# Attention, routed experts and a second expert layer in one kernel: where ak's copy, the routing steps, the low parts of the first weights and the last batch's routing chain are issued

## The chip, the cores and the metric

The kernel runs on one core of one Trainium2 chip. The time is the device time of one execution in microseconds. Its engines are TensorE (PE: matmuls and transposes; its weight loads, PEld, overlap them), VectorE (DVE), ScalarE (ACT), GpSimd (POOL) and SyncE (SP), which here only issues transfers (DMAs). Each engine works through its own instructions in order and waits on semaphores for the others.

## The reference

All inputs are float32. Three stages follow each other; the token of a batch is a row of 512 values (8 heads x 64).

```
# 1. attention with decay: batch 4, heads 8, seq 576, head_dim 64
scores = q @ k.T / 8 + cum[:, None] - cum[None, :]     # cum = cumsum(log(clip(f, 1e-4, 1)))
scores = where(causal, -1e9, scores);  attn = exp(scores - max)
x = (attn / (attn.sum() + 1e-9)) @ v                   # -> 2304 tokens x 512
# 2. one of 8 experts for each token (w1: 512 x 1024, w2: 1024 x 512)
logits = x @ w_gate + modality_bias[modality_id];  e = argmax(logits)
p = exp(logits - max);  gate = (p / (p.sum() + 1e-9))[e]
y = gate * (relu(x @ w1[e]) @ w2[e])
# 3. a dense layer, 2048 wide
h = y @ w_in;  out = maximum(0.01 * h, h) @ w_out
```

## The kernel before

**Precision.** Each float32 operand of a matmul is split into a high part (a copy in the type fp32r) and a low part (the operand less its high part). A product is three matmuls: high x high, high x low, low x high. For an expert's weights `parts(which, k)` makes both: ScalarE copies (`w1h`, `w2h`), VectorE subtracts (`w1l`, `w2l`).

**Attention** runs over 16 head pairs g = 0 to 15, four to a batch. Each pair has five chunks of 128 query rows (the last of 64) and passes through `first`, `last`, `third`, `fourth`. `first(g)` computes the scores of chunks 0 and 1 (`qk01`), transposes the exponentials of chunk 3 of the pair before, prepares the next pair and takes the exponentials of chunks 0 and 1. `last(g)` does chunk 4's scores (`qk4`), `tr(g - 1, 4)`, and attention times values `pv(g - 1, 0)`; `third(g)` chunk 2 and `pv(g - 1, 1)`; `fourth(g)` chunk 3 and the output stage `xout(g - 1)` (two matmul groups into PSUM, normalised by VectorE into `x` and into the gate's partial logits `lp`). Scores lie in the PSUM pool `psc` with two buffers; a chunk's scores can start when the exponentials of two chunks earlier have read theirs. Transposes and output share the pool `pst` with three buffers. `psv`, which `pv` writes and VectorE empties into `xu` and `xub`, has one.

**Preparing a pair.** `raw` holds q (partitions 0 to 63) and k (64 to 127). `prep_hi(g + 2)` rounds both to `aq`, in `fourth(g)`. `prep_lo(g + 1)`, in `first(g)`, copies the high part of k from `aq[64:128]` to `ak[0:64]` (ScalarE), subtracts the low parts (VectorE), and moves 288 KB each by DMA: low q to `bq`, low k to `ak[64:128]`, and the high q from `aq[0:64]` to `aq[64:128]` (which the copy must have read). `qk01(g + 1)` needs all of them. SP issues these in program order, with the stores of finished token rows to `xs` (`store`), the loads of later pairs and those of weights.

**Routing.** When a batch's four pairs are done, `route(b)` (batches 0 to 2) computes each token's expert, gate and rank within its expert, in pieces: it is a generator, each `yield` ends a piece, and `plan` says at which place of which pair the next piece is issued. `route1` (key B) does the table of the first four slots of 128 tokens, and the gathers `xg` of slots 0 and 1. `late_route` is batch 3's. `finish` makes the table of the remaining slots.

**Drain and experts.** `drain(15)` finishes pair 15 and begins slot 0: `wload(0, ...)`, `trx` (transpose a slot's tokens, split into `xh`, `xl`), `gemm1`, `keep` (relu). Then `step(t)` runs over the slots t: `gemm1(t)` and `gemm2(t - 1)` with the weights of the next slot split beside them. Slots 1 to 3 load and split weights only if their expert differs from the slot before (`tc.If`, L1008, a branch that ScalarE and VectorE take). `side` lists what `aside(t, place)` issues between the parts of a step. `gather(K1)`, K1 = 4, belongs to `finish`.

**Order.** `ordered(tc, engines)` keeps program order on the engines named (all five in attention and in the steps). Instructions of two such blocks that follow each other may still be mixed by the scheduler where one runs into the next, as are drain and step 0. `tc.issue_after(i)` queues the block's instructions of i's engine behind i.

Of the kernel before, what the change touches and what calls it, by code (L numbers as in the profile page):

```python
# [19 lines left out]
P = 128  # L20
# [54 lines left out]
def fused(ctx: ExitStack, tc, qk0, qk2, vp, f, mid, wg, mb, w1, w2, w_in, w_out, out):  # L75
# [93 lines left out]

    def parts(which, k):  # L170
        raw, hi, lo = (w2r, WL["2h"], WL["2l"]) if which else (w1r, w1h, WL["1l"])
        nc.scalar.copy(hi[k], raw[k])  # L172
        nc.vector.tensor_tensor(lo[k], raw[k], hi[k].bitcast(F32), ALU.subtract)  # L173
# [25 lines left out]
    with tc.tile_pool(name="pst", bufs=PST, space=PSUM) as pst:  # L199
# [161 lines left out]
        def prep_lo(g):  # L361
            raw, aq, ak = ops[g]
            bq, bk, b4 = bqs[g % NBUF], bks[g % NBUF], bq4[g % NBUF]
            h = aq.bitcast(F32)
            nc.scalar.copy(ak[0:64], h[64:128])
            nc.vector.scalar_tensor_tensor(raw.bitcast(F32R), raw, qs, h, ALU.mult, ALU.subtract)
            nc.sync.dma_start(bq[0:64].bitcast(F32), raw[0:64])
            nc.sync.dma_start(ak[64:128].bitcast(F32), raw[64:128])
            preps.append(nc.sync.dma_start(h[64:128], h[0:64]))
            nc.gpsimd.tensor_copy(b4[0:64, :, :64], raw[0:64, :, 4 * P:])  # L370
            ops[g] = (aq, bq, ak, bk)
# [177 lines left out]
        def route(b):  # L549
# [17 lines left out]
            nc.vector.tensor_tensor(eq, L, mx.unsqueeze(2).to_broadcast(shp), ALU.is_equal)  # L567
            nc.gpsimd.tensor_tensor(lm, L, mx.unsqueeze(2).to_broadcast(shp), ALU.subtract)
            nc.gpsimd.tensor_tensor(eq, eq, rev.unsqueeze(1).to_broadcast(shp), ALU.mult)
            yield  # L570
# [42 lines left out]
        def late_route(b):  # L613
# [18 lines left out]
            nc.vector.tensor_tensor(lm, L, mx.unsqueeze(2).to_broadcast(shp), ALU.subtract)  # L632
# [138 lines left out]
        for b in range(B - 1):  # L771
            a = 4 * b + 5
            places = [(a - 1, "end"), (a, "first")]
            if b < B - 2:
                places += [(a, "idle"), (a, "fourth"), (a + 1, "third"), (a + 1, "idle"), (a + 2, "idle")]
            else:
                places += [(a, "last"), (a, "after"), (a, "third"), (a, "idle"), (a + 1, "idle")]
            for k in places:
                plan.setdefault(k, []).append(b)
        for k in ((13, "end"), (14, "last"), (14, "third"), (15, "first"), (15, "after")):  # L780
            plan.setdefault(k, []).append(B)
# [6 lines left out]
        def first(g):  # L788
            then = qk01(g) if g < NG else None
            cs = [tr(g - 1, 3, (j, )) for j in range(2)] if g else ()  # L790
            for c in cs:
                c()
            if g + 1 < NG:
                prep_lo(g + 1)
# [8 lines left out]
        def last(g):  # L803
            then = qk4(g) if g < NG else None
            if g:
                tr(g - 1, 4, (0, 1))
                routed(g, "last")
# [33 lines left out]
        def drain(g):  # L841
            for k in range(4):
                wload(0, 1, k)
            tr(g, 4, (0, 1))
            for c in [tr(g, 3, (j, )) for j in range(2)]:
                c()
            parts(0, 2)
            pv(g, 0)
            trx(0, pst, "t")
            pv(g, 1)  # L850
            parts(0, 3)
            for k in range(4):
                wload(1, 0, k)
            gemm1(0, 0, 2, psc, "sc")
            xout(g)
            gemm1(0, 2, 3, psc, "sc")
            next(routing[B - 1])
            trx(1, pst, "t")
# [3 lines left out]
        with ordered(tc, MS):  # L862
            prep_hi(1)
            for g in range(NG):
# [23 lines left out]
                if g == NG - 1:  # L888
                    parts(0, 0)
                routed(g, "idle")  # L890
                fourth(g)
                if g == NG - 1:
                    parts(0, 1)
# [87 lines left out]
    with tc.tile_pool(name="rt2", reuse_waits="tile", bufs=1) as rt2, \  # L981
# [87 lines left out]
        def step(t):  # L1069
            nx = t + 1 < NS  # L1070
            if not t:
                split(t, 1, 0)
                split(t, 1, 1)
# [115 lines left out]
        for k, w in (((0, "load"), late), ((0, "b"), late), ((0, "d"), late), ((1, "load"), fini), ((1, "load"), fini), ((1, "a1"), late), ((1, "b"), fini), ((1, "pool"), late), ((1, "d"), fini), ((2, "b"), fini)):  # L1189
# [150 lines left out]
```

## Time and profile before

| | |
|---|---|
| three runs | 889.17, 890.4, 894.68 us; median 890.4 |
| profiled execution | 894.38 us; its span, first to last instruction, 892.7 us; mean granted TensorE clock 0.987 |
| busy, share of the span | PE 96%, DVE 66%, ACT 57%, POOL 20% |
| attention, drain, experts, dense layer | about 0 to 210, 210 to 230, 230 to 482, 482 to 893 us (their edges overlap) |

Times within the profile are counted from the span's start. "Idle before" is the time that an engine stood still ahead of an instruction, with what released it. A granted clock of 1.00 is 2.4 GHz for TensorE, 0.50 is 1.2 GHz. A line number such as L399 is that of the kernel before.

### The profile page before, as it was taken

The page shows a single profiled execution, that of the slowest core. Times are in us where ns is not written, and L with a number is a line of the kernel's source. Part 1 is how long each engine was busy: PE and PEld are TensorE (multiplying, and loading weights), DVE is VectorE, ACT ScalarE, POOL GpSimd, SP SyncE. Part 2 cuts the span into 40 slices and gives each one's busy share as a digit, 9 for nine tenths or more (in the row PEclk, how much of TensorE's full clock was granted, in tenths as well). Part 3 has the DMA queues.
Part 4 walks back from the last instruction along what each step waited for, and adds up shares of the span by engine and source line. Part 5 has one row for each costly group of instructions (what it writes and reads, how often), then busy time and mean ns, then how long its engine had stood idle before and what let it go on. Part 6 is the DMA issues. An engine that isn't in the chain of part 4 may idle for free. (4 is left out here: it accounts for less than half of the span.)

```text
span 892.7 us, 14386 instructions
## 1 busy us (share of the span) xinstructions
PE 854.7 (96%) x4733; PEld 709.8 (80%) x4733; DVE 586.7 (66%) x978; ACT 506.0 (57%) x969; POOL 181.5 (20%) x308
## 2 busy tenths in 40 slices
PE   4999999998899999999999999999999999999996
PEld 3888778886788888888877788888888888888885
DVE  6576667775737999999986373387337853473333
ACT  6777877876247999999975253453223422242221
POOL 5002122251226345444441000000000000001112
PEclk9899999999899999999999999999999999999998
DMA  5676786875268336211421240032001300011111
GB/s 158 199 180 179 193 213 165 218 180 208 78 185 279 96 116 202 67 46 62 119 95 46 78 134 21 1 96 94 0 1 48 119 24 0 1 48 48 48 48 70
DMA packets 33603, 92.92 MB, mean 104 GB/s; under 512 B 7957, under 2 KB 8629, under 8 KB 33522
## 3 DMA queue, kind: packets, MB, share of 16 engines
q1 hardware_dynamic: 28690, 76.70, 29.5%
q0 software_dynamic: 4800, 15.23, 5.0%
q8 instruction: 39, 0.64, 0.3%
q14 instruction: 42, 0.34, 0.1%
q10 hardware_dynamic: 32, 0.01, 0.0%
HBM read 132.09 MB, written 14.99 MB: 165 GB/s over the span
## 5 line engine op out<-in xcount | busy, mean ns | idle before, releaser
L1232 ACT COPY us<-u 128x512 f32<-128x512 f32 (+1 forms) x80 | 43.6, 545 | 162.7 <-PE u L1230 162.6
L1233 DVE SCALAR_TENSOR_TENSOR us<-u,us 128x512 f32<-128x512 f32 (+1 forms) x80 | 51.0, 637 | 126.7 <-ACT us L1232 124.3
L1230 PE MATMUL u<-fxl,whii 128*128 128x512 f32 (+1 forms) x320 | 118.0, 369 | 0.0
L1230 PE MATMUL u<-fxh,wloi 128*128 128x512 f32 (+1 forms) x320 | 117.9, 368 | 0.0
L1230 PE MATMUL u<-fxh,whii 128*128 128x512 f32 (+1 forms) x320 | 116.9, 369 | 0.7 <-ACT fxh L932 0.7
L1250 PE MATMUL a<-whio,gh 128*128 128x512 f32 x280 | 109.7, 392 | 0.0
L1250 PE MATMUL a<-wloo,gh 128*128 128x512 f32 x280 | 109.2, 390 | 0.0
L1250 PE MATMUL a<-whio,gl 128*128 128x512 f32 x280 | 103.2, 390 | 0.0
L173 DVE TENSOR_TENSOR w1l<-w1r,w1h 128x1024 fp32r<-128x1024 f32 x72 | 86.9, 1225 | 16.5 <-ACT w1h L172 16.3
L1260 POOL DMA_INDIRECT out<-acc,tid x18 | 17.8, 987 | 326.7 <-DVE acc L1257 288.0
L173 DVE TENSOR_TENSOR w2l<-w2r,w2h 128x1024 fp32r<-128x1024 f32 x68 | 80.3, 1219 | 0.6 <-ACT w2h L172 0.4
L399 ACT ACTIVATE p<-sc,nm 128x128 f32<-128x128 f32 (+3 forms) x128 | 66.1, 525 | 23.1 <-DVE nm L394 21.1
L1235 ACT CAST gh<-us 128x512 fp32r<-128x512 f32 (+1 forms) x76 | 44.6, 587 | 57.0 <-DVE us L1233 38.1
L172 ACT CAST w1h<-w1r 128x1024 fp32r<-128x1024 f32 x72 | 74.0, 1054 | 1.5 <-PE h L190 1.5
L1236 DVE TENSOR_TENSOR gl<-us,gh 128x512 fp32r<-128x512 f32 (+1 forms) x76 | 49.2, 648 | 37.4 <-ACT gh L1235 35.2
L394 DVE TENSOR_REDUCE nm<-sc 128x2 f32<-128x256 f32 (+1 forms) x64 | 51.0, 817 | 31.7 <-PE sc L390 25.0
L172 ACT CAST w2h<-w2r 128x1024 fp32r<-128x1024 f32 x68 | 69.4, 1051 | 2.6 <-PE y L1037 1.3
L1230 PEld LDWEIGHTS u<-fxh,whii 128*128 128x128 f32 x320 | 60.2, 188 | 11.0 <-ACT fxh L932 0.9
L1230 PEld LDWEIGHTS u<-fxh,wloi 128*128 128x128 f32 x320 | 60.3, 188 | 10.4
L1230 PEld LDWEIGHTS u<-fxl,whii 128*128 128x128 f32 x320 | 60.3, 188 | 10.4
L1037 PE MATMUL y<-w2h,hh 128*128 128x512 f32 x160 | 64.5, 403 | 0.0
L1037 PE MATMUL y<-w2h,hl 128*128 128x512 f32 x160 | 62.8, 393 | 0.0
(318 smaller groups left out, 1854.2 us busy)
## 6 DMA issues: line engine op xcount, KB each, us to landing
w1r<-w SPq DMA_DIRECT2D x88, 512.0 KB
w2r<-w SPq DMA_DIRECT2D x82, 512.0 KB
rwi<-w_in SPq DMA_DIRECT2D x16, 512.0 KB
rwo<-w_out SPq DMA_DIRECT2D x16, 512.0 KB
raw<-qk SPq DMA_DIRECT2D x14, 576.0 KB
vt<-vp SPq DMA_DIRECT2D x16, 320.0 KB
xr<-yd SPq DMA_DIRECT2D x18, 256.5 KB
bk<-aq SPq DMA_DIRECT2D x15, 288.0 KB
```

The lines of the kernel that those rows point to most:

```text
L172: nc.scalar.copy(hi[k], raw[k])
L173: nc.vector.tensor_tensor(lo[k], raw[k], hi[k].bitcast(F32), ALU.subtract)
L394: nc.vector.tensor_reduce(nm, view, axis=AX.X, op=ALU.max, negate=True)
L399: st["exp"] = nc.scalar.activation(pt[:, j, :], view[:, j, :], AF.Exp, bias=nm[:, j:j + 1], scale=1.0, accum_out=sms[g % 3][:, c, j:j + 1])
L1037: nc.tensor.matmul(Yp[t], lhsT=ap[:, k * P:(k + 1) * P], rhs=wp[k // 2][:, k % 2, :], start=(k == 0 and i == 0), stop=(k == NFB - 1 and i ...
L1230: nc.tensor.matmul(ps, lhsT=w[:, c], rhs=x[:, k, :], start=(k == 0 and i == 0), stop=(k == NKB - 1 and i == 2))
L1232: nc.scalar.copy(us, ps)
L1233: nc.vector.scalar_tensor_tensor(us, ps, 0.01, us, ALU.mult, ALU.max)
L1235: nc.scalar.copy(gh, us)
L1236: nc.vector.tensor_sub(gl, us, gh.bitcast(F32))
L1250: nc.tensor.matmul(A[b][i], lhsT=x[:, c], rhs=w, start=(first and m == 0), stop=(last and m == 2))
L1260: d = nc.gpsimd.indirect_dma_start(out=out[:, :], out_offset=bass.IndirectOffsetOnAxis(ap=tid[:, c:c + 1], axis=0), in_=Y[b, i], in_offset ...
```

## The change

Four parts. ak's copy and the DMA within `aq` leave `prep_lo` for `prep_k`, which for pairs 2 to 14 is issued in `last`, behind the exponentials of chunks 0 and 1 and the copies of chunk 4. In `route`, `eq x rev` goes from GpSimd to VectorE, a `yield` goes, and the places in `plan` are set anew. `parts` is cut into `high` and `low`; in `drain` the low parts are issued behind the output stage and `pv(15, 0)` ahead of chunk 3's transposes; `trx(1)` comes ahead of the last batch's first routing piece. The first two splits of w2 are queued behind the end of that piece on VectorE, and the pieces of `late_route` and `finish` get later places in `side`.

```diff
--- before.py
+++ after.py
@@ -167,10 +167,20 @@
         n = NTOK if t >= K1 else NTOK - S
         nc.gpsimd.indirect_dma_start(out=xg[t % 2], out_offset=None, in_=xs[:n, :], in_offset=bass.IndirectOffsetOnAxis(ap=m[:, i:i + 1], axis=0), bounds_check=n - 1, oob_is_err=False)
 
+    def tiles(which, k):
+        return [t[k] for t in ((w2r, WL["2h"], WL["2l"]) if which else (w1r, w1h, WL["1l"]))]
+
+    def high(which, k):
+        raw, hi, _ = tiles(which, k)
+        nc.scalar.copy(hi, raw)
+
+    def low(which, k):
+        raw, hi, lo = tiles(which, k)
+        nc.vector.tensor_tensor(lo, raw, hi.bitcast(F32), ALU.subtract)
+
     def parts(which, k):
-        raw, hi, lo = (w2r, WL["2h"], WL["2l"]) if which else (w1r, w1h, WL["1l"])
-        nc.scalar.copy(hi[k], raw[k])
-        nc.vector.tensor_tensor(lo[k], raw[k], hi[k].bitcast(F32), ALU.subtract)
+        high(which, k)
+        low(which, k)
 
     def trx(t, pool, tag):
         ps = pool.tile([P, 512], F32, tag=tag, name=f"tx{t}")
@@ -362,13 +372,17 @@
             raw, aq, ak = ops[g]
             bq, bk, b4 = bqs[g % NBUF], bks[g % NBUF], bq4[g % NBUF]
             h = aq.bitcast(F32)
-            nc.scalar.copy(ak[0:64], h[64:128])
             nc.vector.scalar_tensor_tensor(raw.bitcast(F32R), raw, qs, h, ALU.mult, ALU.subtract)
             nc.sync.dma_start(bq[0:64].bitcast(F32), raw[0:64])
             nc.sync.dma_start(ak[64:128].bitcast(F32), raw[64:128])
+            nc.gpsimd.tensor_copy(b4[0:64, :, :64], raw[0:64, :, 4 * P:])
+
+        def prep_k(g):
+            raw, aq, ak = ops[g]
+            h = aq.bitcast(F32)
+            nc.scalar.copy(ak[0:64], h[64:128])
             preps.append(nc.sync.dma_start(h[64:128], h[0:64]))
-            nc.gpsimd.tensor_copy(b4[0:64, :, :64], raw[0:64, :, 4 * P:])
-            ops[g] = (aq, bq, ak, bk)
+            ops[g] = (aq, bqs[g % NBUF], ak, bks[g % NBUF])
 
         st = {}
         XA, XB = 3 * P, P + 64
@@ -565,9 +579,8 @@
             eq = t3("eq")
             lm = t3("lm")
             nc.vector.tensor_tensor(eq, L, mx.unsqueeze(2).to_broadcast(shp), ALU.is_equal)
+            nc.vector.tensor_tensor(eq, eq, rev.unsqueeze(1).to_broadcast(shp), ALU.mult)
             nc.gpsimd.tensor_tensor(lm, L, mx.unsqueeze(2).to_broadcast(shp), ALU.subtract)
-            nc.gpsimd.tensor_tensor(eq, eq, rev.unsqueeze(1).to_broadcast(shp), ALU.mult)
-            yield
             m2 = rsp.tile([P, NC], F32, tag="m2", name=f"m2{b}")
             red(m2, eq, ALU.max)
             oh = oall[:, b * NC:(b + 1) * NC, :]
@@ -629,7 +642,7 @@
             nc.vector.tensor_tensor(eq, eq, rev.unsqueeze(1).to_broadcast(shp), ALU.mult)
             nc.vector.tensor_reduce(m2, eq, axis=AX.X, op=ALU.max)
             nc.vector.tensor_tensor(oh, eq, m2.unsqueeze(2).to_broadcast(shp), ALU.is_equal)
-            nc.vector.tensor_tensor(lm, L, mx.unsqueeze(2).to_broadcast(shp), ALU.subtract)
+            st["late"] = nc.vector.tensor_tensor(lm, L, mx.unsqueeze(2).to_broadcast(shp), ALU.subtract)
             yield
             rk = ranks(b, oh, pmx, "tx")
             yield
@@ -770,14 +783,14 @@
         plan = {}
         for b in range(B - 1):
             a = 4 * b + 5
-            places = [(a - 1, "end"), (a, "first")]
+            places = [(a - 1, "end"), (a, "idle" if b < B - 2 else "first")]
             if b < B - 2:
-                places += [(a, "idle"), (a, "fourth"), (a + 1, "third"), (a + 1, "idle"), (a + 2, "idle")]
+                places += [(a, "end"), (a + 1, "third"), (a + 1, "idle"), (a + 2, "idle")]
             else:
-                places += [(a, "last"), (a, "after"), (a, "third"), (a, "idle"), (a + 1, "idle")]
+                places += [(a, "last"), (a, "third"), (a, "idle"), (a + 2, "first")]
             for k in places:
                 plan.setdefault(k, []).append(b)
-        for k in ((13, "end"), (14, "last"), (14, "third"), (15, "first"), (15, "after")):
+        for k in ((13, "end"), (14, "idle"), (14, "idle"), (15, "last"), (15, "after")):
             plan.setdefault(k, []).append(B)
 
         def routed(g, at):
@@ -788,9 +801,12 @@
         def first(g):
             then = qk01(g) if g < NG else None
             cs = [tr(g - 1, 3, (j, )) for j in range(2)] if g else ()
+            if g < 2:
+                prep_lo(g + 1)
+                prep_k(g + 1)
             for c in cs:
                 c()
-            if g + 1 < NG:
+            if 2 <= g < NG - 1:
                 prep_lo(g + 1)
             store(1 + (g > 12))
             routed(g, "first")
@@ -804,6 +820,8 @@
             then = qk4(g) if g < NG else None
             if g:
                 tr(g - 1, 4, (0, 1))
+                if 2 <= g < NG - 1:
+                    prep_k(g + 1)
                 routed(g, "last")
                 pv(g - 1, 0)
             if then:
@@ -841,21 +859,27 @@
         def drain(g):
             for k in range(4):
                 wload(0, 1, k)
+            low(0, 0)
             tr(g, 4, (0, 1))
-            for c in [tr(g, 3, (j, )) for j in range(2)]:
+            high(0, 1)
+            pv(g, 0)
+            low(0, 1)
+            cs = [tr(g, 3, (j, )) for j in range(2)]
+            for c in cs:
                 c()
-            parts(0, 2)
-            pv(g, 0)
             trx(0, pst, "t")
+            high(0, 2)
             pv(g, 1)
-            parts(0, 3)
+            low(0, 2)
+            high(0, 3)
+            gemm1(0, 0, 2, psc, "sc")
+            low(0, 3)
             for k in range(4):
                 wload(1, 0, k)
-            gemm1(0, 0, 2, psc, "sc")
             xout(g)
             gemm1(0, 2, 3, psc, "sc")
+            trx(1, pst, "t")
             next(routing[B - 1])
-            trx(1, pst, "t")
             gemm1(0, 3, 4, psc, "sc")
             keep(0)
 
@@ -886,11 +910,9 @@
                 if not g:
                     last(g)
                 if g == NG - 1:
-                    parts(0, 0)
+                    high(0, 0)
                 routed(g, "idle")
                 fourth(g)
-                if g == NG - 1:
-                    parts(0, 1)
                 routed(g, "end")
             drain(NG - 1)
         att.close()
@@ -1069,8 +1091,9 @@
         def step(t):
             nx = t + 1 < NS
             if not t:
-                split(t, 1, 0)
-                split(t, 1, 1)
+                with tc.issue_after(st["late"].ins):
+                    split(t, 1, 0)
+                    split(t, 1, 1)
             keepg(t)
             if t + 2 < NS and t + 2 != K1:
                 gather(t + 2)
@@ -1186,7 +1209,7 @@
 
         fini = finish()
         late = routing[B - 1]
-        for k, w in (((0, "load"), late), ((0, "b"), late), ((0, "d"), late), ((1, "load"), fini), ((1, "load"), fini), ((1, "a1"), late), ((1, "b"), fini), ((1, "pool"), late), ((1, "d"), fini), ((2, "b"), fini)):
+        for k, w in (((1, "load"), late), ((1, "b"), late), ((1, "pool"), late), ((1, "pool"), late), ((1, "d"), fini), ((1, "d"), fini), ((2, "load"), late), ((2, "load"), fini), ((2, "b"), fini), ((2, "d"), fini)):
             side.setdefault(k, []).append(w)
         with ordered(tc, MS2):
             for t in range(NSTAT):
```

## Rows read from the trace of the kernel before

**Rows 1.** The page's first part: engine, busy us, share of the span, instructions.
```profile
PE 854.7 (96%) x4733; PEld 709.8 (80%) x4733; DVE 586.7 (66%) x978; ACT 506.0 (57%) x969; POOL 181.5 (20%) x308
```

**Rows 2.** TensorE's waits, whole span: for what, us in total, times, longest.
```profile
PE sc L384 <- ACT p L399: 7.3, 13, 0.6
...
PE rk L605 <- DVE oall L631: 1.7, 1, 1.7
...
PE pv L485 <- DVE xu L491: 1.4, 2, 0.9
...
PE h L190 <- DVEq L1008: 0.7, 1, 0.7
```

**Rows 3.** Stretches: length, busy time by engine, granted clock, DMA share, GB/s.
```profile
22.90:29.75 6.85, 6.85 (x32) 6.58 (x32) 3.80 (x5) 3.52 (x10) 0.86 (x3) 0.50 0.93 293
190.14:193.55 3.41, 1.91 (x18) 1.60 (x18) 1.99 (x5) 1.94 (x8) 2.69 (x11) 1.00 0.95 223
...
214.07:217.49 3.42, 3.17 (x14) 1.63 (x14) 1.46 (x2) 2.71 (x6) 0.00 (x0) 0.50 0.02 5
...
231.09:237.92 6.83, 6.10 (x19) 4.74 (x18) 5.57 (x23) 1.03 (x4) 5.28 (x11) 0.50 0.16 42
...
233.00:445.00 212.00, 212.00 (x1032) 175.09 (x1031) 188.91 (x242) 173.56 (x232) 92.20 (x77) 0.99 0.39 123
```

**Rows 4.** TensorE's timeline, pairs 7, 8, 15, drain: start, us, instruction, idle before.
```profile
104.62 0.44 PE L384 MATMUL sc<-ak,aq 128*128 128x384 f32 x1 [0.56 <-ACT p L399]
...
110.88 0.30 PE L384 MATMUL sc<-ak,aq 128*128 128x128 f32 x1
...
197.88 0.32 PE L384 MATMUL sc<-ak,aq 128*128 128x128 f32 x1
...
213.19 0.41 PE L463 MATMUL pt<-ident,p 128*128 128x128 f32 x2 [2.33 <-DVE lp L512]
...
226.16 0.60 PE L178 MATMUL tx<-ident,xg 128*128 128x128 f32 x4
```

**Rows 5.** ScalarE's timeline in pair 7.
```profile
101.68 1.15 ACT L365 CAST ak<-aq 64x1152 fp32r<-64x1152 f32 x1
...
104.36 0.21 ACT L399 ACTIVATION_READ_ACCUMULATOR p<-sc,nm 128x1 f32 x1
104.45 0.76 ACT L465 COPY tt<-pt 128x384 f32<-128x384 f32 x2
```

**Rows 6.** SP's timeline in pair 14: transfers as they are issued.
```profile
190.56 0.71 SPq L369 DMA_DIRECT2D aq<-aq  x1
191.32 1.20 SPq L672 DMA_DIRECT2D xs<-x  x1
192.57 1.05 SPq L670 DMA_DIRECT2D xs<-x  x1
```

**Rows 7.** Stretches of pairs 7, 8 and 14 (columns as in rows 3).
```profile
104.00:110.00 6.00, 5.44 (x49) 4.55 (x48) 3.45 (x9) 4.42 (x16) 0.00 (x0) 1.00 0.98 239
116.00:122.50 6.50, 5.93 (x55) 4.86 (x52) 2.81 (x4) 4.92 (x16) 0.00 (x0) 1.00 0.96 234
190.00:198.30 8.30, 6.80 (x62) 5.92 (x58) 5.21 (x17) 5.76 (x19) 5.66 (x24) 1.00 0.99 249
```

**Rows 8.** VectorE's timeline in pair 13.
```profile
177.56 0.20 DVE L530 TENSOR_REDUCE mx<-lgs 128x5 f32<-128x40 f32 x1 [0.95 <-POOL lgs L561]
...
178.92 0.55 DVE L491 COPY xu<-pv 128x384 f32<-128x384 f32 x1
```

**Rows 9.** VectorE's timeline from pair 15's last scores into the first expert.
```profile
209.27 1.23 DVE L173 TENSOR_TENSOR w1l<-w1r,w1h 128x1024 fp32r<-128x1024 f32 x1 [2.09 <-ACT w1h L172]
210.41 1.22 DVE L394 TENSOR_REDUCE nm<-sc 128x2 f32<-128x1024 f32 x1
...
225.61 0.80 DVE L625 TENSOR_REDUCE lgs<-lp 128x40 f32<-128x320 f32 x1
...
232.31 0.34 DVE L645 TENSOR_SCALAR jall<-pf 128x5 f32<-128x5 f32 x1 [0.89 <-DVEq L1008]
```

## The prediction

> **What bounds the kernel now.** I read the page's first part, then what TensorE waited for, then busy time and clock by stretch, then the timelines of the four places that the diff touches. TensorE is busy for 854.7 of 892.7 us [rows 1], so an edit can pay only where TensorE stands still or runs at the lower clock. From 233 to 445 us it has no gap (212.00 of 212.00 busy) [rows 3]: a later start there would not be made up, and an earlier one is kept down to the end, VectorE (188.91 of 212) following. Ahead of it lie 13 short waits on the exponentials, 7.3 us together, one of about a microsecond on `xu`, one of 2.33 us in the drain, and 1.7 and 0.7 us when the experts begin [rows 2, 4]. Three stretches run at a granted clock of 0.50, that is at 1.2 GHz: 6.85, 3.42 and 6.83 us [rows 3]. Each comes behind one TensorE wait of 1.7 to 2.4 us; the waits of 0.55 and 0.95 us together, inside 190.14 to 193.55, were followed by none (1.00 there).
>
> **ak's copy behind the exponentials.** In pair 7 the exponentials of chunks 0 and 1 end at 104.36 + 0.21 = 104.57, and `qk(7, 2)` starts at 104.62 after 0.56 idle, so it was wanted at 104.06 [rows 4, 5]. With the copy (1.15, with its gap 1.17) taken from ahead of them they end at 103.40: the wait goes whole. Late next on ScalarE would be the fourth exponential: after the two copies of chunk 4 (0.76, to 104.2) and ak's copy (to 105.35) it ends near 106.4, and its PSUM buffer is wanted at 107.84 - 0.56 = 107.3. Covered by 0.9. Pairs 0 and 1 keep the copy ahead and show no such wait. Pairs 2 to 12: 11 x 0.56 = 6.2 us saved. Pairs 13 and 14 follow below.
>
> With the copy moves a DMA: the high part of q, 288 KB, into `h[64:128]`, for the next pair. It must wait for ScalarE's copy, so it now leaves SP at 105.4 or later, about a microsecond behind its old place; and in `first` the store of routed rows is now issued ahead of it on the same queue. Where there is no store it has 4.9 us till the next pair, and is hidden (a microsecond later is a microsecond of slack gone, no more). In pairs 7, 8, 11 and 12 a store of 513 KB goes ahead: 3 x 288 + 513 = 1377 KB, or 1.41 MB, must have moved. At 239 GB/s from 104.0 [rows 7] that is 109.9, against a need at 110.88 - 0.56 = 110.32 [rows 4]; in pair 8, at 234 GB/s from 116.0, 122.0 against about 122.5. What the last pieces need beyond that I can't see. Bounds: 0 and 0.56 each (the old start); I take 0.25: 4 x 0.25 = 1.0 lost.
>
> Pair 14 is the bad one. There both stores (1026 and 128 KB) are issued behind the old place of the copy [rows 6], and now ahead of it. All four transfers are 3 x 288 + 1154 = 2018 KB = 2.07 MB, and 249 GB/s over 8.30 us from 190.0 [rows 7] is just that: the last lands at 198.3 or later. `qk01(15)` started at 197.88 and, with both waits of pair 14 gone (0.55 and 0.95), is wanted at 196.4. Bounds of the new wait: 0 (the copy overtakes the stores) and 3 us. I take 2.3, nearest to the byte count plus some tail: pair 15 starts at 198.7, which is 0.8 later than before, in place of 1.5 earlier.
>
> **Routing in one step, and the new places.** For batches 0 and 1 the five small VectorE steps move to "idle", behind `xub` and ahead of the next maxima, where VectorE waits for TensorE anyway (1.5 us in pair 8, which has no step of routing). They cost 5 x 0.22 = 1.1: nothing; with the cover gone it would be 1.1 each. In batch 2 they stay at (13, "first"), ahead of the chunk-4 maximum (0.75) and of `xu`. There VectorE waits 0.95 for GpSimd's logits and begins at 177.56; now mx, eq, eq x rev, m2 and oh run as one chain to 178.6, the maximum to 179.3, `xu` to 179.85, where it ended at 178.92 + 0.55 = 179.47 [rows 8]. TensorE, 0.57 earlier at that point, waits at `pv` for it: pair 13 saves nothing and loses 0.35. Batch 3's table: steps 2 and 3 leave (14, "last") for (14, "idle"), which takes VectorE's wait for GpSimd from ahead of `xu`; that is the 0.95 counted in pair 14. The five `lall` operations go from (14, "idle") to (15, "first"), 0.9 us that end before the chunk-4 scores are there: nothing. SP reads `ei` for the first expert's weights when GpSimd has written it, and that chain doesn't move.
>
> **Drain.** VectorE sits 2.09 us behind `w1h`, subtracts (1.23), and only then takes pair 15's last maxima (at 210.41) [rows 9]. The scores are there at 208.65, so without `low(0, 0)` ahead of it the maxima and pair 14's output stage behind them run 1.75 us earlier, and TensorE's 2.33 us wait [rows 4], which is for that output stage's PSUM buffer, shrinks to 0.6. The low parts that follow have 1.2 us each against gemm1 steps of 1.4 and come in time by my reckoning (the fourth by 3 us). From 213.19 to the transposes of the second tile's end at 226.5 are 13.3 us; less 0.74 of short waits and 1.6 for the half clock at 214.07 to 217.49 (3.17 busy) [rows 3, 4], 11.0. So `trx(1)` ends at 213.19 - 1.75 + 11.0 + 0.3 (for `tt`) = 222.7, 3.8 earlier.
>
> **Last batch's chain in one piece.** `trx(1)` now stands ahead of that chain on VectorE: `xh` 0.6, `xl` 0.7, so the chain begins at 224.0, not 225.61 [rows 9]. It is eight operations, 0.83 + 7 x 0.23 = 2.44; the two subtractions of `w2`, now held behind it, 2 x 1.2; then 0.89 until VectorE is past the branch on whether the second slot's weights change, where TensorE waits at its first `w1l`: 224.0 + 2.44 + 2.4 + 0.89 = 229.75. Before, this point was 232.31 (TensorE resumed at 232.28), with xl, the rank wait and five steps of the ranks in between. So 2.5 us are gained, while TensorE waits longer in that place (some 1.2 and 3.4 us, against 1.7 and 0.7 [rows 2]). The half clock of 231.09 to 237.92, whose end fell into gapless work, I keep at its price: 0, with bounds of -1.7 and +1.7. The remaining steps of both chains move to later places, where VectorE is little used (t = 1 to 3 load no new weights); the gather of slot 4 leaves GpSimd some 7 us later, 6 ahead of its transposes, behind no other gather; SP reads `ei` of slot 4 after VectorE wrote it. Nothing; if this cover failed, 1 to 3 us.
>
> **The clock.** A wait of 2.3 us ahead of pair 15 is like those that were followed by 3.42 to 6.85 us at 0.50 [rows 3]; in gapless work a half-clock stretch costs half its length, 1.7 to 3.4. With 3 chances in 4: 2.0. The Trainium skill ("TensorE: Matmul & The Clock Gate", Part 1) says that for modelling such a ramp is under 1% of a kernel's span and not to be fitted; by that this term would go and the gain below be 6.8. Here 1% is what is to be told, and the trace's three stretches cost about half of 17 us, so the row's price stands.
>
> **Sum**, against the profiled execution's own 894.38 us (span 892.7 and 1.7 around it): 6.2 - 1.0 - 0.35 - 0.8 = 4.05 by pair 15; - 2.0; + 2.55 by the first expert; = 4.6 earlier, 889.8. That execution is 4.0 above the median of the three runs, 890.4; against the median, 885.8.
>
> **Rivals.**
> (a) The copy lands in time. The Trainium skill ("DMA: Bandwidth & Descriptors", Queues, rings and completion order) has one DMA engine take a ring's descriptors in order, yet calls completion not first-in-first-out; no row here shows overtaking. If the copy isn't held by the stores, pair 14 keeps its 1.5, pairs 7 to 12 their 1.0, and no half clock comes: 4.6 + 2.3 + 1.0 + 2.0 = 9.9, or 880.5. For it: before, the three 288 KB copies took under 5 us. Against: the byte counts. 0.22.
> (b) Slower. The copy lands so late in all five pairs with a large store that each wait is followed by a half-clock stretch: each wait some 1.7 us or more, plus 1.7 to 3.4 us. Five times 3.5 to 4 more than the old start, less what is saved: 18 - 8 = 10 us slower, 900. It decides where the copy lands 1.7 us after TensorE wants it; the byte counts have pairs 7 and 8 at 0.4 ahead. 0.05.
> (c) The move does not take the wait away, because the exponentials then wait for the maxima (VectorE's second one ends 0.1 us behind the copies that precede them) or the copy for another. 6.2 fall to about 1: 4.6 - 5 = 0, 890.5. The first rows speak against: 1.17 is taken away and 0.56 needed. 0.10.
> (d) My forecast, with the long wait ahead of pair 15: 885.8, own range 882 to 890. 0.63.
>
> **How the numbers follow.** The predicted time is that of (d). (a) holds 0.22 at 880.5, so the low end goes to 878; the unknown costs (pairs 7 to 12 up to 2.2, pair 14 up to 0.7, the clock 1.4 and 1.7 more) reach 892 to 893. About 1% of 890.4, or 8.9 us, is what a measurement of this kernel can tell from no change. Faster than 881.5: most of (a) and a little of (d), 0.27. Slower than 899.3: part of (b) and mishaps in the experts' start, 0.05. Within: 0.68.
>
> **What would show it.** The waits of `sc` on the exponentials gone from 13 to near 0; at the start of pairs 8, 9, 12 and 13 small waits on the DMA into `aq`, at pair 15 one of about 2 us and behind it a granted clock of 0.50; `pv` waiting 0.5 to 1 us on `xu` in pair 13 and no longer in pair 14; in the drain a wait of 0.6 in place of 2.33; the first `w1l` of the second slot 2.5 us nearer to `qk01(15)` than now. I am wrong if pair 15 starts without a DMA wait (then faster), or if VectorE's branch comes later than 2.4 us behind the two subtractions (then slower).

## The result, and the profile after

| | before | after |
|---|---|---|
| median of four runs each | 890.31 us (889.17 to 894.68) | 901.17 us (900.59 to 904.10) |
| profiled execution, its span | 894.38, 892.7 us | 901.43, 899.7 us |
| mean granted clock in it | 0.987 | 0.986 |

The changed kernel is slower: ratio 1.0119, 95% interval 1.0079 to 1.016, where 885.8 us was forecast. The page's first part of the changed kernel beside [rows 1]: TensorE is busy 4.3 us longer and the span is 7.0 us longer.

```profile
span 899.7 us, 14367 instructions
...
PE 859.0 (95%) x4733; PEld 713.7 (79%) x4733; DVE 588.5 (65%) x981; ACT 505.5 (56%) x969; POOL 180.9 (20%) x305
```

TensorE's waits from 45 to 275 us after the change, to be laid beside [rows 2]. Lines have moved: L384 of before is L398, L485 is L499, L190 is L200, L1008 is L1030.

```profile
PE sc L398 <- DMA aq<-aq: 12.1, 6, 5.5
PE h L200 <- DVEq L1030: 2.1, 1, 2.1
PE tp L731 <- DVE xl L190: 1.4, 1, 1.4
PE h L200 <- ACTq L1030: 1.2, 1, 1.2
PE pt L477 <- DVE lp L526: 0.7, 1, 0.7
PE pv L499 <- DVE xu L505: 0.5, 1, 0.5
```

The 13 waits on the exponentials (7.3 us) are gone, as meant, and so is the wait on `oall`; in their place stand 12.1 us on the copy within `aq`, in six pairs, and 1.4 us at a place that had no wait, the table's matmuls. The timeline of TensorE shows where (start, us, instruction, idle before):

```profile
36.66 0.32 PE L398 MATMUL sc<-ak,aq 128*128 128x128 f32 x1
...
51.27 0.43 PE L398 MATMUL sc<-ak,aq 128*128 128x128 f32 x1 [2.88 <-DMA aq<-aq]
...
104.60 0.44 PE L398 MATMUL sc<-ak,aq 128*128 128x384 f32 x1
...
113.18 0.30 PE L398 MATMUL sc<-ak,aq 128*128 128x128 f32 x1 [2.17 <-DMA aq<-aq]
...
125.79 0.30 PE L398 MATMUL sc<-ak,aq 128*128 128x128 f32 x1 [0.75 <-DMA aq<-aq]
...
203.21 0.44 PE L398 MATMUL sc<-ak,aq 128*128 128x128 f32 x1 [5.46 <-DMA aq<-aq]
...
219.22 0.41 PE L477 MATMUL pt<-ident,p 128*128 128x128 f32 x2 [0.68 <-DVE lp L526]
...
236.34 1.22 PE L200 MATMUL h<-w1l,xh 128*128 128x512 f32 x2 [2.13 <-DVEq L1030]
...
262.16 1.45 PE L731 MATMUL tp<-h,lall 128*128 128x42 bf16 x20 [1.40 <-DVE xl L190]
```

Read beside [rows 4]: `qk(7, 2)`, which waited 0.56 us at 104.62, starts at 104.60 with no wait. But pair 3 starts 2.88 us late, pair 8 by 2.17, pair 9 by 0.75, pair 12 by 0.56, pair 13 by 0.28 and pair 15 by 5.46. Pair 15 starts at 203.21 in place of 197.88. Pairs 2 to 14 together took 160.34 us (37.54 to 197.88) and now take 166.55 (36.66 to 203.21); from there to the end it was 694.8 us and is now 696.5. So 6.2 of the span's 7.0 us were lost between the starts of pairs 2 and 15, and 1.7 behind that, where the lower clock of pair 15 (worth 2.6 us, see the clock below) lies too: drain and experts by themselves lost nothing in sum. The 0.9 gained ahead of pair 2 need not be the change's: before's execution has a stretch at 1.2 GHz there, at 22.90 [rows 3], this one has none, and e1 and e10, whose code there is that of the changed kernel, have one again (e1 from 23.43, e10 from 23.07).

The same stretches as in [rows 3] and [rows 7] (length, busy time by engine, granted clock, DMA share, GB/s):

```profile
51.27:54.69 3.42, 3.42 (x16) 3.32 (x17) 0.90 (x2) 0.07 (x1) 0.00 (x0) 0.51 0.85 294
113.18:116.60 3.42, 3.42 (x28) 3.25 (x29) 1.82 (x3) 1.40 (x5) 0.15 (x1) 1.00 0.60 154
201.50:208.40 6.90, 5.20 (x24) 5.13 (x25) 1.83 (x7) 1.62 (x5) 0.00 (x0) 0.51 1.01 365
235.75:242.60 6.85, 6.26 (x25) 5.04 (x26) 3.38 (x4) 0.82 (x2) 2.04 (x2) 0.51 0.15 42
263.00:266.40 3.40, 3.40 (x16) 2.68 (x14) 0.20 (x1) 0.00 (x0) 1.59 (x4) 0.50 0.98 330
...
190.50:203.21 12.71, 7.25 (x65) 5.83 (x61) 6.21 (x18) 7.28 (x19) 6.20 (x29) 0.93 0.92 230
```

Four stretches at 1.2 GHz (half clock from here on), where before's execution had three: behind the waits in pairs 3 and 15, where the second slot begins, and behind the table's wait. The last line is for the forecast's byte count: from the first transfer of pair 14 to the start of pair 15, when the copy had landed, 12.71 us x 230 GB/s = 2.92 MB were moved, and the four transfers up to and with the copy hold 2.07 MB.

SP's timeline, pairs 2 and 14 (issues of transfers), beside [rows 6]:

```profile
42.31 0.79 SPq L229 DMA_DIRECT2D mbs<-mb  x1
43.20 3.94 SPq L233 DMA_DIRECT2D midi<-mid  x4
47.19 0.71 SPq L234 DMA_DIRECT2D midi<-mid  x1
48.00 0.55 SPq L384 DMA_DIRECT2D aq<-aq  x1
...
191.70 0.79 SPq L685 DMA_DIRECT2D xs<-x  x1
192.53 1.86 SPq L683 DMA_DIRECT2D xs<-x  x1
194.57 1.29 SPq L384 DMA_DIRECT2D aq<-aq  x1
195.96 1.92 SPq L256 DMA_DIRECT2D vt<-vp  x1
```

In pair 14 the copy is issued at 194.57, behind both stores, where it was issued at 190.56, ahead of them. In pair 2 it stands behind six small loads, the modality table and the tokens' modality (`gload(1)`), which keep SP from 42.31 to 47.90.

### The profile page after: what moved, and what is told of

It is laid out like the page before. It is cut to its first block, busy times and chain, and to the rows that moved or that the text cites. A ratio compares the mean times of both kernels' runs of the same rounds, so it can differ in the third digit from the quotient of the medians.

```text
span 899.7 us, 14367 instructions
## 1 busy us (share of the span) xinstructions
PE 859.0 (95%) x4733; PEld 713.7 (79%) x4733; DVE 588.5 (65%) x981; ACT 505.5 (56%) x969; POOL 180.9 (20%) x305
## 5 line engine op out<-in xcount | busy, mean ns | idle before, releaser
L489 ACT COPY tt<-pt 128x256 f32<-128x256 f32 (+2 forms) x96 | 45.3, 520 | 39.4 <-PE pt L487 39.2
```

Source lines behind the costliest of these rows:

```text
L489: return lambda: nc.scalar.copy(o, ps[:, :len(js) * nb * P].rearrange("p (j b q) -> p j b q", b=nb, q=P))
```

## The experiments

Four theories, two and two. The copy within `aq` is late because of what stands ahead of it in SP's queue (order), or because it now leaves behind ScalarE's copy, whatever stands ahead (lateness). And what is lost behind pair 15 lies in the last batch's chain and its new places (experts), or more narrowly at the table, in the PSUM buffer that it shares (bank). Ratios are those to before, run on the same chip beside the kernel; a kernel is compared with another through these.

| | what it is | us (median) | ratio, 95% interval |
|---|---|---|---|
| after | the change | 901.17 | 1.0119, 1.0079 to 1.0160 |
| e2 | before with the copy's move alone | 902.36 | 1.0128, 1.0109 to 1.0146 |
| e5 | after, copy within aq on ScalarE's queue | 902.46 | 1.0115, 1.0090 to 1.0140 |
| e9 | after, modality loads behind the copy | 898.90 | 1.0076, 1.0050 to 1.0101 |
| e10 | after, pair 14's stores behind it | 894.03 | 1.0013, 0.9997 to 1.0030 |
| e1 | after, all stores and loads behind it | 884.79 | 0.9926, 0.9903 to 0.9949 |
| e3 | after, table in another PSUM bank | 900.38 | 1.0109, 1.0084 to 1.0134 |
| e4 | e1 and e3 | 882.30 | 0.9902, 0.9885 to 0.9920 |
| e6 | e1 with the last batch's chain as before | 880.18 | 0.9872, 0.9846 to 0.9897 |
| e7 | e4 with the drain as before | 884.76 | 0.9919, 0.9891 to 0.9947 |
| e8 | e4, branch ahead of w2's low parts | 877.06 | 0.9835, 0.9816 to 0.9854 |
| e11 | e8, ak's copy back ahead of the exponentials | 884.14 | 0.9909, 0.9893 to 0.9925 |
| e12 | e8 with the routing as before | 879.88 | 0.9855, 0.9836 to 0.9875 |

**e1: the copy ahead of stores and loads.**

```diff
# first(g)
-            store(1 + (g > 12))
             routed(g, "first")
# last(g)
                     prep_k(g + 1)
+                store(1 + (g > 12))
# attention's loop: gload(1) goes from behind first(2) to behind last(2)
```

> The changed kernel, with one thing reordered on SP: the copy within aq is issued ahead of the row stores, and in pair 2 ahead of the loads of the modality ids, all else as changed. Order theory (the copy is late because of what is issued ahead of it on its queue): the six waits on it, 12.1 us, fall below 1 us, the lower clock of pairs 3 and 15 goes (1.7 and 2.6 us), and the time is 882 to 887. Lateness theory (it is late because ScalarE's copy now comes a microsecond later and the transfers are full anyway, in whatever order): half the waits stay, 892 to 896. Experts theory (most of the loss lies in the drain and the first slots): 899 or more.

Measured 884.79, 17 us below the changed kernel by the ratios. ScalarE's copy and the copy within `aq` stand where the change put them; only SP's order differs. SP's timeline in pair 14 of this kernel:

```profile
185.47 0.46 SPq L384 DMA_DIRECT2D aq<-aq  x1
185.98 0.59 SPq L685 DMA_DIRECT2D xs<-x  x1
186.61 1.38 SPq L683 DMA_DIRECT2D xs<-x  x1
```

Its waits on the copy are 3.0 us in four pairs, one of them (1.61) at pair 1, whose copy the experiment doesn't touch, and pair 15 has none. The three that are left, 1.4 us in pairs 4, 8 and 13, are more than the 1 us expected. Being a microsecond later costs no more than these; standing behind other transfers is the loss.

**e2: the copy's move alone.** Before, with `prep_k` at its new place and nothing else.

```diff
# before.py: prep_lo loses ak's copy and the copy within aq to prep_k, as in the change
             if g:
                 tr(g - 1, 4, (0, 1))
+                if 2 <= g < NG - 1:
+                    prep_k(g + 1)
```

> The kernel before, with the first part of the change alone: ak's copy and the copy within aq behind the exponentials. Order theory: the waits of the scores on the exponentials go (7.3 us and more), and the six waits on the copy come, 11 to 13 us, with a lower clock behind the longest two; 896 to 900, so that this part alone is the whole loss. If the loss came from the other parts: 882 to 886.

Measured 902.36: this part alone makes the whole loss, and a little more than the 896 to 900 expected of it. Its TensorE's waits:

```profile
PE sc L388 <- DMA aq<-aq: 13.7, 7, 4.3
...
PE pv L489 <- DVE xu L495: 2.8, 3, 1.6
```

The second line stands at 1.4, 2, 0.9 in [rows 2]: with the old routing, `xu` comes late three times instead of twice, and by up to 1.6 us, once TensorE no longer waits for the exponentials. e12 comes back to it.

**e5: another queue for the copy.**

```diff
-            preps.append(nc.sync.dma_start(h[64:128], h[0:64]))
+            preps.append((nc.scalar if g >= 3 else nc.sync).dma_start(h[64:128], h[0:64]))
```

> The changed kernel; only the copy within aq (pairs 3 to 15) leaves from ScalarE's queue in place of SP's. The stores and the modality loads keep their places, so the same bytes are under way when it is issued. Order theory (it was late because it stood behind them in one queue, waiting for its turn on SP and in the rings): the six waits of 12.1 us on aq fall to under 3 us together, as when it was issued ahead of them; 884 to 889, the upper end if issuing it costs ScalarE time ahead of the next exponentials. Bandwidth theory (what is late is the number of bytes under way, whatever the queue): pairs 8, 9 and 15 keep waits of 1 to 5 us, 8 us or more together; 895 to 901.

Measured 902.46, with 14.8 us of waits on the copy in eleven pairs, the longest 2.9. A queue of its own doesn't save the copy: what leaves ahead of it makes it late, in whichever queue. So of the two theories it is bandwidth, and worse than I had it (895 to 901): pairs without a store wait too. ScalarE's timeline and SP's, pair 6 of this kernel:

```profile
95.24 1.15 ACT L383 CAST ak<-aq 64x1152 fp32r<-64x1152 f32 x1
96.42 0.47 ACTq L384 DMA_DIRECT2D aq<-aq  x1
```

```profile
94.45 1.51 SPq L377 DMA_DIRECT2D ak<-raw  x1
96.05 0.55 SPq L265 DMA_DIRECT2D raw<-qk  x1
```

SP no longer stops for ScalarE's copy, so the 576 KB load for a later pair (L265), which in the changed kernel stands behind the copy on SP, goes out 0.37 us ahead of it, and both share the engines. It is so for each of the ten such loads from pair 3 to pair 12, by 0.2 to 1.9 us, and in the changed kernel the same load follows the copy every time. Of pairs 3 to 15 only pairs 3 and 14 don't wait, and no such load goes ahead of their copies. That this load makes the frequent waits is read from these times; no run holds it back alone. The Trainium skill ("DMA: Bandwidth & Descriptors", Issuing engines are not separate DMA queues) says that transfers started from several engines run on the same 16 DMA engines and interleave, and that a second queue saves issue time alone. This run agrees: longest wait 2.9 in place of 5.5, their sum 14.8 in place of 12.1.

**e9 and e10: the loads alone, pair 14's stores alone.**

```diff
# e9: only gload(1) goes behind last(2).  e10, in first(g):
-            store(1 + (g > 12))
+            if g != 14:
+                store(1 + (g > 12))
# and in last(g), behind prep_k:
+                if g == 14:
+                    store(1 + (g > 12))
```

> The changed kernel; only the modality column and its five loads (ahead of the copy within aq in pair 2) are issued behind that copy; the stores stay ahead. If pair 3's wait of 2.88 us is for them: it is gone, and with it the half-clock stretch behind it (1.7 us): 896 to 898 against 901.2. Rival (the copy of pair 3 is late for its bytes, not for SP's time): the wait stays over 2 us, 900 to 902.

> The changed kernel; only pair 14's two stores (1026 and 128 KB) are issued behind the copy within aq; those of pairs 7, 8, 11 and 12 and the modality loads stay ahead. If these two stores are pair 15's whole wait of 5.46 us: it is gone, and the half clock behind it (6.8 us, worth some 2.6): 893 to 894 against 901.2. Rival (the wait is there without them, or the stores then hold the first expert's weights by as much): 897 or more.

Both came out as the first theory had it, e9 a microsecond higher. By the ratios the loads cost 3.8 us (the intervals of e9 and the changed kernel overlap, so this one rests on the trace) and the two stores 9.4; 17.2 less these leaves 4.0 for pairs 8, 9, 12 and 13, whose waits sum to 3.76. TensorE's timeline of e9 at the start of pair 3, then of e10 at pair 3 and at pair 15:

```profile
48.59 0.32 PE L398 MATMUL sc<-ak,aq 128*128 128x128 f32 x1
```

```profile
52.27 0.33 PE L398 MATMUL sc<-ak,aq 128*128 128x128 f32 x1 [2.81 <-DMA aq<-aq]
...
200.46 0.32 PE L398 MATMUL sc<-ak,aq 128*128 128x128 f32 x1
```

The wait of pair 3 goes with the loads and that of pair 15 with the two stores, and each stays when only the other's transfers are moved (e9's pair 15 waits 5.58 us).

**e3 and e4: the table in another PSUM bank.** `tp` takes the buffer of pool `pm0` instead of that of `trx`.

```diff
-tb = table(rt2, N2, NTL, stk, pmx, "tx", h2p)
+tb = table(rt2, N2, NTL, stk, pm0, "th", h2p)
```

> The changed kernel, with the table matmuls of the later slots in another PSUM bank than the transposes of slot 3's tokens. Bank theory (TensorE waits 1.4 us there because VectorE has not yet emptied the one bank that both use): the wait goes, and with it the lower clock of 263 to 266 us; 2.5 to 3.2 us less, 898 to 899. If the table's own inputs are late: no change, 901.

> Both reorderings in one kernel. If the two costs are independent, as order and bank theory have it: the sum, 879 to 884, faster than either kernel. If removing the waits in attention only moves the wait to the experts' start: 886 to 890.

In both, the wait of 1.4 us and the half clock behind it are gone from the trace. In time e3 tells nothing from after (1.0109 and 1.0119, intervals overlapping; 898 to 899 us were expected), since its waits on the copy were as long again; e4 is 2.1 us below e1 by the ratios, whose intervals still overlap. So the wait is shown to be the buffer's, and its price in time is not told from noise. The half clock is not part of that price every time: e1 has the same wait of 1.40 us, and the full clock behind it.

```profile
245.49:248.90 3.41, 3.41 (x29) 2.80 (x29) 0.20 (x1) 0.00 (x0) 0.85 (x3) 1.00 0.93 339
```

From TensorE's 0.68 us wait in the drain to the end, e1's profile has 679.1 us and e4's 676.25. Of these 2.9 us 1.4 are the wait; e1 also has a half-clock stretch from 463.74 to 467.15, long past the table, that e4 has not.

**e6: the last batch's chain as before the change.**

```diff
# drain
-            trx(1, pst, "t")
             next(routing[B - 1])
+            trx(1, pst, "t")
# step(0): the two splits of w2 without issue_after; side as in before
```

> The version with the copy issued ahead of the stores (884.8 us), with the last part of the change undone: the last batch's chain in its old pieces and places, the first two splits of w2 not held behind it, the table back in its old place. As predicted (part worth 2.5 us, nothing lost later): 887.3. Experts theory (part gains some 2 us at the first w1l of the second slot and loses 2.5 at the table's matmuls, which wait for VectorE behind the transposes in the same PSUM buffer): no wait of 1.4 on xl at the table, 884 to 886, no difference that can be told.

Measured 880.18, 4.8 us below e1 by the ratios and below what either theory had (887.3, 884 to 886): the part is no gain, and costs more than the 1.4 us at the table. TensorE's timeline of this kernel:

```profile
216.84 0.19 PE L618 MATMUL rk<-oall,before 128*128 128x32 bf16 x1 [1.71 <-DVE oall L644]
...
219.24 1.22 PE L200 MATMUL h<-w1l,xh 128*128 128x512 f32 x2
...
225.56 0.39 PE L1061 MATMUL y<-w2h,hh 128*128 128x512 f32 x1
```

Against its own drain wait (202.50) the first `w1l` of the second slot comes 16.74 us later; in e1 17.15 (203.76 to 220.91). The first `gemm2` matmul comes after 23.06 us; in e1 after 24.60 (to 228.36). One wait of 1.71 us on the chain stands against 1.16 + 2.14 us on the branch of ScalarE and VectorE. To the end, e6's profile has 676.1 us from its drain wait and e1's 679.1: 3.0, which are the 1.5 of the first `gemm2` and the 1.4 of the table.

**e8: the branch ahead of w2's low parts.** What those two waits are made of is VectorE's timeline of the changed kernel, beside [rows 9]:

```profile
231.12 0.69 DVE L190 TENSOR_TENSOR xl<-tx,xh 128x512 fp32r<-128x512 f32 x1 [1.83 <-ACT xh L189]
231.72 0.72 DVE L638 TENSOR_REDUCE lgs<-lp 128x40 f32<-128x320 f32 x1
...
233.87 2.35 DVE L179 TENSOR_TENSOR w2l<-w2r,w2h 128x1024 fp32r<-128x1024 f32 x2
236.43 2.43 DVE L179 TENSOR_TENSOR w2l<-w2r,w2h 128x1024 fp32r<-128x1024 f32 x2 [0.21 <-DVEq L1030]
```

VectorE waits 1.83 us for `xh`, though the chain behind it could start (its operand `lp` was done at 229.28), and 2.35 us of subtractions that the first `gemm2` doesn't need for another 9 us (245.07) lie ahead of the branch for which TensorE waits. e8 takes the chain ahead of `trx(1)` and the two splits behind the branch.

```diff
 def step(t):
-            if not t:
-                with tc.issue_after(st["late"].ins):
-                    split(t, 1, 0)
-                    split(t, 1, 1)
...
-            if t:
-                split(t, 1, 0)
-                split(t, 1, 1)
+            split(t, 1, 0)
+            split(t, 1, 1)
# drain: next(routing[B - 1]) ahead of trx(1, pst, "t")
```

> The same version (882.3 us); for the first slot the two low parts of w2 are issued behind VectorE's branch on the second slot's weights, no longer ahead of it, and the routing piece ahead of the second slot's transposes. If TensorE's waits of 1.2 and 2.1 us when the second slot begins are for those two subtractions (2 x 1.2) ahead of the branch: both shrink to under 1 together, 879 to 880. Rival (the low parts of w2 are needed as early as the branch, by gemm2 of the first slot): a wait of as much on w2l in their place, 882 to 883.

Measured 877.06, the fastest here and below the 879 to 880 expected, 14.7 us below before by its ratio. The two moves were made together, so what each brings is not separated. TensorE's timeline:

```profile
217.31 0.74 PE L200 MATMUL h<-w1h,xh 128*128 128x512 f32 x2 [1.11 <-ACT hs L205]
...
220.21 0.19 PE L618 MATMUL rk<-oall,before 128*128 128x32 bf16 x1
...
224.28 0.40 PE L1061 MATMUL y<-w2h,hh 128*128 128x512 f32 x1
```

Both branch waits are gone; 1.11 us, on ScalarE's `hs` for the first slot, come to light in their place. The first `gemm2` matmul follows the drain's wait (203.56) by 20.72 us. No wait on `w2l` appears.

**e7: the drain as before.** Low parts ahead of the output stage, in e4.

```diff
# drain
-            low(0, 0)
             tr(g, 4, (0, 1))
-            high(0, 1)
-            pv(g, 0)
-            low(0, 1)
             for c in [tr(g, 3, (j, )) for j in range(2)]:
                 c()
+            parts(0, 2)
+            pv(g, 0)
# and so on; parts(0, 0) and parts(0, 1) back in pair 15
```

> The version with the copy ahead of the stores and the table in the other PSUM bank (882.3 us), with the drain as before the change (low parts of w1 ahead of the output stage). As predicted (drain worth 1.75 us): TensorE's wait in the drain is 2.0 to 2.4 again, 884.0 without and 885.7 with a half-clock stretch behind it. Rival (the drain's gain is taken back at the branch, where TensorE waits for VectorE anyway): waits ahead of the second slot's w1h and w1l shorter by as much, 882 to 883.

TensorE's wait in the drain is 2.33 us again. Measured 884.76, 2.5 above e4 in medians and 1.5 by the ratios, whose intervals overlap, so the time can't tell; in the trace the gain, 2.33 less 0.68, is of the predicted size (1.75).

**e11 and e12: what the two attention parts are worth with nothing in their way.**

```diff
# e11, first(g):
             if 2 <= g < NG - 1:
                 prep_lo(g + 1)
+                prep_k(g + 1)
# e12: eq x rev on GpSimd, the yield and plan as in before
```

> The best version so far (877.1 us) with ak's copy and the copy within aq back in their place ahead of the exponentials of chunks 0 and 1; all else, stores behind the copies too, stays. What the move is worth by itself once nothing stands ahead of the copy: by the prediction 11 x 0.56 + 0.55 in pair 14 = 6.7, so 883.8; by the undisturbed pairs of the changed kernel, 0.66 each, 8 to 9, so 885 to 886. Rival (the waits on the exponentials are mostly taken back elsewhere): 879 to 880.

> The best version so far (877.1 us) with the routing as before the change: eq x rev on GpSimd, the extra step, the old places. By the prediction the new routing gains 0.95 in pair 14 and loses 0.35 in pair 13, and nothing elsewhere: 877.7, no difference that can be told. Rival (the chain in one step delays the maxima and xu in more pairs than 13): 875 to 876.

e11 measured 884.14, 6.6 us above e8 by the ratios, where 6.7 was predicted for the move. Its TensorE waits from 45 to 260 us have the old line back:

```profile
PE sc L398 <- ACT p L413: 6.8, 12, 0.6
```

e12 measured 879.88; 0.9855 against 0.9835, the intervals overlap, so the time can't tell. The trace can: pairs 2 to 14 take 155.98 us in it and 153.13 in e8, with these waits of TensorE from 45 to 260 us:

```profile
PE pv L499 <- DVE xu L505: 3.0, 3, 1.6
```

They are 0.74 (at 77.77), 0.74 (125.39) and 1.57 (186.55), pairs 5, 9 and 14, where e8 has one of 0.51. These 2.5 us are most of the 2.85; e12 also waits 1.0 us longer on the copy, which the routing doesn't touch. Neither theory had it: by these two traces the new routing is worth more than was predicted, not less.

## Why the prediction was wrong, step by step

The forecast gained 4.6 us against before's profile and the trace lost 7.0. Up to pair 15 it is 9.4 us off (4.05 earlier forecast, 5.33 later measured); from there to the second slot's first `w1l` 0.7 us better than forecast (34.40 to 33.13 us, forecast 0.55 shorter with the half clock); behind that 2.9 worse (660.4 to 663.4, forecast equal).

**Failed: "Bounds of the new wait: 0 (the copy overtakes the stores) and 3 us. I take 2.3, nearest to the byte count plus some tail".** The wait is 5.46. I counted the bytes issued up to and with the copy, took a rate, and had little left for the tail. The trace records a transfer's landing in 16 steps. The 2.07 MB at the 230 GB/s of this stretch are 9.0 us, so 199.5 from 190.50; the copy's first step is at 199.48 and its last, for which TensorE waits, at 203.07. In before's pair 14 the 16 steps lie within 0.4 us (194.98 to 195.37), in e1's within 0.8. The tail behind the stores, 3.6 us, is what I had too small. In these 3.6 us pieces of later transfers moved, of `vt` and of the first expert's weights (told by their sizes, 2560 and 4096 bytes); they are nearly all of the 0.85 MB above 2.07. The byte count gave the landing of the first part, and I took it nearly for the last. e10 puts 9.4 us on this one place; the wait and the half clock behind it are 8.1 of them. The Trainium skill ("DMA: Bandwidth & Descriptors", Queues, rings and completion order) says that completion is not first-in-first-out for one issuing engine. I cited that for the case in which the copy overtakes the stores; nothing of the kind is seen here, for by their last steps the transfers landed as they were issued: the stores at 201.66 and 201.88, the copy at 203.07, `vt` at 203.63.

**Failed: "Where there is no store it has 4.9 us till the next pair, and is hidden."** Pair 2 has no store, and has six small loads, which keep SP for 5.6 us ahead of the copy; pair 3 waits 2.88 us and runs 3.42 us at half clock behind it, 4.6 us together. e9 gives 3.8 us for it. The queue that a DMA is moved past was read for the stores alone.

**Failed in size: "Bounds: 0 and 0.56 each (the old start); I take 0.25."** Pairs 8, 9, 12 and 13 wait 2.17, 0.75, 0.56 and 0.28: 3.76 for 1.0. Three lie above or at the upper bound, for which there was no reason but the old start.

**Failed: "Nothing; if this cover failed, 1 to 3 us."** The late chain's places were read for engines and queues and not for the PSUM buffer. The table's matmuls now follow `trx` into the same single buffer, and TensorE waits 1.40 for VectorE to empty it (e3, e4), in the profiled execution with 3.40 us of half clock behind, which e1 hasn't.

**The late chain: the working held, the place didn't.** `w1l` comes 17.12 us behind the drain's wait after the change (18.3 worked out), 19.09 before. But e7, with the old drain and the new chain, has 19.12, and e6, new drain and old chain, 16.74: the whole gain at this point is the drain's. And it was the wrong point to sum at: what was moved behind it, the ranks among it, still had to be done, and the first `gemm2` comes 1.5 us later in e1 than in e6. "So 2.5 us are gone" should have been a loss: with the table some 3 us by the profiles of e1 and e6, 4.8 by their ratios.

**Right: the exponentials' wait.** Pair 4, which nothing disturbs, takes 11.46 us (64.53 to 75.99) where it took 12.12 (61.80 to 73.92), 0.66 less where 0.56 was worked out. e11 gives 6.6 us for the whole, 6.7 predicted.

**Right: the drain's wait** (0.68, predicted 0.6; before 2.33) and a wait on `xu` in pair 13 (0.46, predicted 0.5 to 1) and none in pair 14. **Too small: the routing.** For batches 0 and 1 I priced only what its steps cost and found nothing; in e12 the old routing costs 0.74 us each in pairs 5 and 9, and in pair 14 1.57, 0.6 more than before, now that the exponentials' waits are gone.

**The clock.** 2.0 us were forecast behind pair 15. The stretch there at 0.50, from 203.21 to 208.40, costs 2.6 (half of its length, as in the forecast); pair 3's costs 1.7 and the table's 1.7. Before's profiled execution had two stretches (22.90 and 214.07) that this one doesn't, so that half clock in all costs about 9.4 us (half of 3.42 + 5.19 + 6.85 + 3.40) where it cost 8.5. It is a loss that follows waits, and not every time. The Trainium skill ("TensorE: Matmul & The Clock Gate", Part 1) puts the ramp under 1% of a typical span; all stretches together are 9.4 of 899.7 here, a little over it. Left out of the sum, as that rule has it, the term would have put the forecast further off: the gain would have been 4.05 + 2.55 = 6.6, where the working says 6.8.

**The rivals.** (b), 900 us, gave the measured time, and its direction, the copy late behind the stores, is the one that happened. That its number fits is luck, for its condition is not met: of the five pairs only 8 and 15 waited 1.7 us or more, and only pair 15 was followed by half clock; pairs 3, which (b) doesn't have, and 15 make most of the price, and the chain adds to it. It got 0.05 because "the byte counts have pairs 7 and 8 at 0.4 ahead", the same step that failed above. (a) and (c) are out: the copy landed behind the stores, and the exponentials' wait did go.

**Open.** Why the copy's 16 steps lie 3.6 us apart behind the stores and under 1 us apart without them is not shown: the trace doesn't tell which of the 16 DMA engines moved which piece.

## What to carry to other kernels

When an instruction is moved, list everything that its queue issues between the old place and the new, small loads too, and keep a DMA that the next stage needs ahead of stores that nobody waits for: here that order alone was worth 17 us. A byte count over a rate gave the landing of a transfer's first part here; its last part, which the next stage waits for, came 3.6 us later. Sum a chain's gain at a point behind which nothing of it is left, and of what is put ahead of a branch for which TensorE waits, ask whether anyone needs it sooner.

## What was not expected of the hardware

Parts of a transfer landed 3.6 us apart, and meanwhile pieces of transfers issued later in its queue moved: 2.92 MB in all for the 2.07 MB up to and with it. Whole transfers of the one queue still landed there in the order of issue. Giving the copy a queue of its own made its waits shorter but more frequent (11, 14.8 us in all), while the queue that it left ran ahead.

The half clock doesn't go by the length of the one wait ahead of it. Pair 8's wait of 2.17 us was followed by a granted clock of 1.00 in the changed kernel (113.18 to 116.60, above); its wait of 2.31 us in e10, at 114.36, by this:

```profile
115.20:118.62 3.42, 3.42 (x18) 3.33 (x17) 2.27 (x3) 1.22 (x3) 0.00 (x0) 0.50 0.35 78
```

And the table's 1.40 us were followed by 3.40 us at 0.50 in the changed kernel, but by 1.00 in e1 (above) and in e5, e9 and e10, which have the same wait.
